# A slot-attention and feed-forward kernel: the first 520 pieces of its hand-written order, rearranged

## The chip, the cores and the metric

The kernel runs on one core of a Trainium2 chip. The metric is the device time of one execution in microseconds (us). TensorE (PE) multiplies matrices, VectorE (DVE), ScalarE (ACT) and GpSimd (POOL) do the element-wise work, and SyncE (SP) issues all the transfers (DMA). PEld is TensorE's loading of weights, which runs beside its products.

## What is computed

For each of 8 batches, 8 heads and 576 positions, phi (32 numbers) is turned into weights by a softmax. These weights pool k and v into 32 slots for each head; q attends to the slots, and the result, 4608 rows of 512, goes through a feed-forward layer.

```python
a = np.exp(phi - np.max(phi, axis=2, keepdims=True))
a = a / (np.sum(a, axis=2, keepdims=True) + 1e-09)
k_m = np.einsum('bhsm,bhsd->bhmd', a, k)
v_m = np.einsum('bhsm,bhsd->bhmd', a, v)
scores = scale * np.matmul(q, k_m.transpose(0, 1, 3, 2))
attn = softmax(scores)                      # over the 32 slots
x = rows of np.matmul(attn, v_m)            # 4608 x 512
h = x @ w_in                                # 4608 x 2048
out = (0.5 * h * (1.0 + erf(h / sqrt(2)))) @ w_out
```

## The kernel before

The whole program is a list of pieces, the string ORDER. Each word is a call, such as `h.0.3.1` or `dA.4.1:p`; a suffix after the colon picks the engine (d VectorE, a ScalarE, p GpSimd) or a PSUM pool (x, y). The pieces are traced in that order, and then every instruction is chained behind the one before it on its engine, so each engine works strictly in the order of the list. Engines wait for each other only where data or buffers ask for it.

Batch b's work is this. `Lphi`, `Lkv`, `Lkv0`, `Lq` load; `amax` and `aexp` (VectorE, ScalarE) do phi's softmax; `at` transposes it on TensorE and `atc` copies it out of PSUM; `slots.b.g.w` pools k (w 0) or v (w 1) for head group g; `km` scales the slots, `slotsT` transposes them and `kT` copies them. For batch 0 the scores are made in three parts: `n_score` (TensorE), `n_max`, `n_sub`, `n_exp`, `n_sum`, `n_inv`, `n_mul`, then `n_T` turns them and `n_hi` and `n_lo` split them into two parts, p_hi and p_lo. Later batches use `score`, `sT`, `max`, `sub`, `exp`, `sum`, `inv`, `mul`, `pT`, `ph`, `pl`. `Up.b.f.n` (line 695) multiplies v's slots by n blocks of 128 columns of w_in; `Uh` and `Ul` split the product into U. `h.b.f.half` (line 957, six products of 288 columns) gives 128 of the 2048 hidden units for half a batch; `gelu.b.f.half` (lines 965 to 968), `gh` and `gl` (line 974) follow, and `p.b.f` (line 988, twelve products of 512 columns) adds this block's share of the output into four PSUM banks, which `o.b.j.f` empties. `W.n` is n products of a block of ones (line 1058) whose result nobody reads.

The weights arrive as pairs of words and are decoded in the kernel. For block f, `.0` is w_in and `.1` is w_out: `Lwi.f` and `Lwo.f` load both into one tile raw_f; `dX` (lines 396 and 398) and `dY` (line 401) make two summands, `dA` adds them, and for w_out `dE` and `dF` split the sum into wo_hi and wo_lo.

```python
def dec_a(f, k):
    w, x = word_of(k, f), top_of(f, k).rearrange("p (c n) -> p c n", c=ND)
    e = eng("p")
    if e is nc.vector:
        w, x = upper(w), upper(x)
    e.tensor_tensor(w, w, x, op=ALU.add)
```

On VectorE an addition touches only the upper 16 bits; those of w_in lie 4 bytes apart, those of w_out 8, since `word_of` leaves w_out in raw_f.

Five buffers (the tag "U") serve the raw tiles and the U tiles, so that a load of block f waits until `dF` of an earlier block, or the last `h` of an earlier U, has let a buffer go. `h` has two PSUM buffers: an `h` waits for the gelu of the last but one. `score`, `Up`, `slots` and `at` of batch 1 share one pair of PSUM banks. phi has one buffer, so that batch 1's `Lphi` waits for the last `at` of batch 0.

Of the kernel before, what the change touches and what calls it, by code (L numbers as in the profile page):

```python
# [39 lines left out]
gelu.0.0.1 gh.0.0:a dY.3.1 Ul.0.2 gelu.0.1.1 dF.1 h.0.2.0 dY.2.1 Up.0.3.1 km.1.0:a gl.0.0  # L40
gh.0.1:a dA.3.1:p dX.2.1:d dY.4.1 gl.0.1 dX.4.0:a p.0.0 dX.4.1:d slots.1.1 dA.4.1:p
dE.3:a Lwi.5 h.0.2.1 dA.2.1:d Uh.0.3:a dY.4.0 Ul.0.3 Lq.1.0 dF.3 dE.2:a km.1.1:d slotsT.1
gelu.0.2.0 dE.4:a dY.5.0 kT.1:a Lwo.5 h.0.3.0 dA.4.0:d dX.5.0:d score.1.0 Lwi.7 dA.5.0:d
gelu.0.2.1 dF.4 gh.0.2:a sT.1.0.0 Lwi.6 gelu.0.3.0 Lq.1.1 h.0.3.1 sT.1.0.1 Lwo.6 Lphi.2.1
Up.0.4.2 max.1.0 p.0.1 dX.5.1:d Uh.0.4:a dY.5.1 gelu.0.3.1 dA.5.1:p sub.1.0 Ul.0.4
exp.1.0 h.0.4.0 dY.7.0 h.0.5.1 dE.5:a dF.2 gh.0.3:d gl.0.2 gelu.0.4.0 gelu.0.5.1
score.1.1 dX.6.1:a dY.6.0 dX.6.0:d p.0.2 dY.6.1 sum.1.0 dX.7.0:a gl.0.3 Lwo.8 h.0.5.0
Lwi.8 h.0.4.1 inv.1.0 dF.5 Up.1.0.4 gelu.0.5.0 gelu.0.4.1 mul.1.0 dA.6.0:p pT.1.0 dY.8.1
sT.1.1.1 Uh.1.0:a ph.1.0:a gh.0.4:a dA.6.1:p p.0.3 sT.1.1.0 dX.8.1:a dE.6:a dA.7.0:d
Lwo.7 max.1.1 Ul.1.0 gl.0.4 Up.0.6.2 Uh.0.6:a gh.0.5:d dY.7.1 sub.1.1 Ul.0.6 dX.7.1:a  # L50
dA.7.1:p gl.0.5 dF.6 p.0.4 exp.1.1 Lwo.9 h.0.6.1 Lwi.9 h.0.6.0 gelu.0.6.1 p.0.5 sum.1.1
pl.1.0 Lwi.11 h.0.7.1 dE.7:d dA.8.1:p gelu.0.6.0 inv.1.1 gelu.0.7.1 dY.9.0 h.1.0.0
dX.8.0:a Lwo.10 mul.1.1 h.0.7.0 gelu.1.0.0 gh.0.6:d gelu.0.7.0 pT.1.1 gl.0.6 ph.1.1:a
dY.8.0 Lwo.11 p.0.6 dF.7 Lwi.13 dX.9.1:d pl.1.1 gh.0.7:a dY.9.1 dX.9.0:a dA.9.1:p Lwi.10
gl.0.7 dE.8:d h.1.1.1 h.1.1.0 h.1.0.1 p.0.7 gelu.1.1.1 gelu.1.1.0 h.1.3.1 dY.11.0 dF.8
gh.1.1:d h.1.3.0 dA.8.0:d gl.1.1 dE.9:a h.1.2.1 gelu.1.0.1 o.0.2.7:a dX.11.0:d h.1.2.0
Up.1.4.4 gh.1.0:a dY.10.1 gelu.1.3.1 Lwo.14 dF.9 gl.1.0 dA.9.0:d gelu.1.3.0 o.0.0.7:a
dX.10.1:d o.0.3.7:d dY.10.0 o.0.1.7:a p.1.0 Lwo.13 dX.10.0:a dA.10.1:p gelu.1.2.1
gelu.1.2.0 dA.11.0:d Uh.1.4:a dE.10:a dA.10.0:d Ul.1.4 dY.14.1 dY.13.1 dY.11.1 h.1.7.1
h.1.4.1 Lwi.15 Up.0.8.4 Lwi.14 Lwi.12 p.1.1 dX.11.1:d dX.13.1:d dF.10 gh.1.2:a gl.1.2  # L60
Lwo.12 dY.15.0 dA.11.1:p p.1.2 Lphi.2.0 dX.13.0:d gelu.1.4.1 h.1.4.0 dX.14.0:d gh.1.3:a
h.1.5.1 dE.11:d h.1.5.0 gl.1.3 gelu.1.7.1 gelu.1.4.0 dY.14.0 gh.1.4:d p.1.3 gelu.1.5.0
gelu.1.5.1 h.1.7.0 gelu.1.7.0 Lwo.15 dF.11 h.1.6.1 dY.13.0 dY.12.0 gl.1.4 gh.1.5:d
Uh.0.8:a gl.1.5 gh.1.7:a h.1.6.0 Ul.0.8 dX.14.1:d dA.14.0:p p.1.4 gelu.1.6.0 dA.13.1:d
gelu.1.6.1 gl.1.7 p.1.5 h.0.8.1 gh.1.6:a gl.1.6 gelu.0.8.1 dX.12.0:d h.0.8.0 gelu.0.8.0
dY.12.1 h.0.10.0 p.1.6 dA.12.0:p h.0.9.0 dA.14.1:p dE.14:a p.1.7 h.0.10.1 h.0.9.1
dA.13.0:d dX.12.1:d Lkvu.2.0 gh.0.8:d h.0.11.0 dE.13:a dF.14 dA.12.1:p gelu.0.9.0 gl.0.8
o.1.1.7:a gelu.0.10.0 dE.12:a Lq.2.0 o.1.0.7:a gelu.0.10.1 dX.15.0:d o.1.2.7:d gelu.0.9.1
Up.0.12.2:x dA.15.0:d gh.0.9:a o.1.3.7:a gelu.0.11.0 amax.2.1 h.0.11.1 Uh.0.12:a gl.0.9
amax.2.0 dF.13 gelu.0.11.1 dX.15.1:a dF.12 dY.15.1 p.0.8 p.0.9 Ul.0.12 gh.0.10:d  # L70
h.0.12.1:y gh.0.11:a h.0.12.0:y h.0.13.0:x gelu.0.12.0 gl.0.10 gelu.0.12.1 h.0.13.1:x
dg.2 dA.15.1:d Up.0.14.2:y gl.0.11 gelu.0.13.0 gh.0.12:d Up.1.8.4:x p.0.10 gelu.0.13.1
Uh.1.8:a Uh.0.14:d gl.0.12 Ul.0.14 Ul.1.8 Lphin.2 gh.0.13:d p.0.11 h.0.14.0:y aexp.2.1
dE.15:a h.0.15.0:x h.0.14.1:y dF.15 aexp.2.0 h.1.8.0:y Lphi.3.0 Lphi.3.1 pn.2 gelu.0.14.0
gelu.0.14.1 gl.0.13 h.0.15.1:x gelu.0.15.0 h.1.8.1:y gelu.0.15.1 p.0.12 h.1.9.0:x
gh.0.14:d gh.0.15:d gl.0.14 gelu.1.8.0 gelu.1.8.1 aadd.2 anorm.2 Lkvu.2.1 gl.0.15 p.0.13
h.1.9.1:x gelu.1.9.0 p.0.14 gelu.1.9.1 gh.1.8:d gl.1.8 anexp.2 amax.3.0 amax.3.1 aexp.3.0
aexp.3.1 wg p.0.15 gh.1.9:d gl.1.9 dg.3 pn.3 h.1.10.0:y o.0.0.15 Lkv5.2 o.0.1.15
h.1.10.1:y gelu.1.10.0 o.0.2.15 h.1.11.0:x gelu.1.10.1 o.0.3.15 h.1.11.1:x gelu.1.11.0
# [1087 lines left out]
```

## Time and profile before

| | |
|---|---|
| median of 3 runs | 695.67 us (695.54 to 695.82) |
| profiled execution | 696.96 us, of which the span of its instructions is 695.2 us |
| TensorE busy in the span | 681.5 us (98%) |
| VectorE, ScalarE, GpSimd busy | 376.5, 298.8 and 40.0 us |
| TensorE's granted clock over the span | 0.996 of full speed |

Full speed is 2.4 GHz, and half of it, 1.2 GHz, is the other level. The busy time of TensorE is counted from modelled ends of its products, so a busy engine is not always at its peak. An engine's idle time costs something only if the work that sets the end waits for it.

### The profile page before, as it was taken

Reading aid. Unit: us, or ns where it says so; the run is one execution under the profiler, and the core shown is the slowest. Engines: PE = TensorE matmul, PEld = TensorE weight load, DVE = VectorE, ACT = ScalarE, POOL = GpSimd, SP = SyncE. Lnnn points to the kernel's source line nnn. Section 1 sums busy time; section 2 is a strip of 40 time slices with the busy share of each in tenths; the row PEclk is TensorE's granted clock in tenths of the full one; section 3 lists DMA queues with packets and bytes.
Section 4 is the critical chain, followed back from the end, with each engine's and each line's share of the span. In section 5 each row is a group of like instructions: output and inputs, shape, how many; then the busy total and the mean of one; then the engine's idle time right before and its main releaser. Section 6 shows DMA issues by size and latency. Waiting matters only on the chain.

```text
span 695.2 us, 12223 instructions
## 1 busy us (share of the span) xinstructions
PE 681.5 (98%) x4934; PEld 572.9 (82%) x4934; DVE 376.5 (54%) x708; ACT 298.8 (43%) x699; POOL 40.0 (6%) x31
## 2 busy tenths in 40 slices
...
GB/s 337 336 280 147 212 169 123 53 50 175 114 111 132 168 190 50 62 124 67 35 17 75 115 76 35 16 62 36 35 0 61 18 34 1 1 60 1 1 1 75
DMA packets 27865, 63.57 MB, mean 91 GB/s; under 512 B 2592, under 2 KB 6432, under 8 KB 27808
## 3 DMA queue, kind: packets, MB, share of 16 engines
...
q14 instruction: 18, 0.15, 0.1%
...
## 4 chain that ended last, share of the span: by engine, by line
PE 94%; DVE 2%; DMA 1%; ACT 1%; issue 0%; SPq 0%; DVEq 0%; ACTq 0%
PE acc L988 50%; PE h L957 29%; PE tacc L988 5%; PE pu L695 4%; PE psc L618 1%; PE psc L695 1%; DMA q<-qT 1%; PE pk L618 1%; PE psc L714 0%; PE pw L1058 0%; PE pk L603 0%; DVE U L316 0%; PE pt L524 0%; ACT L965 0%; DVE gl_t L983 0%
## 5 line engine op out<-in xcount | busy, mean ns | idle before, releaser
L957 PE MATMUL h<-p_hi,U 128*128 128x288 f32 x1024 | 217.2, 296 | 0.5 <-DVE U L316 0.3
L957 PEld LDWEIGHTS h<-p_hi,U 128*128 128x128 f32 x1024 | 168.7, 188 | 5.2 <-ACT gh L307 0.9
L988 PE MATMUL acc<-wo_hi,gh 128*128 128x512 f32 x512 | 161.2, 395 | 0.0
L307 DVE CAST gh<-gf 128x512 fp32r<-128x512 f32 x114 | 49.4, 433 | 204.5 <-PE acc L988 192.7
L988 PE MATMUL acc<-wo_lo,gh 128*128 128x512 f32 x512 | 158.6, 390 | 0.0
L988 PE MATMUL acc<-wo_hi,gl 128*128 128x512 f32 x512 | 158.6, 390 | 0.0
L957 PE MATMUL h<-p_lo,U 128*128 128x288 f32 x512 | 150.3, 295 | 0.0
L965 ACT ACTIVATE gf<-h 128x288 f32<-128x288 f32 x128 | 52.6, 412 | 174.2 <-PE h L957 149.7
L988 PEld LDWEIGHTS acc<-wo_hi,gh 128*128 128x128 f32 x512 | 92.9, 188 | 30.8 <-issue 14.7
L988 PEld LDWEIGHTS acc<-wo_hi,gl 128*128 128x128 f32 x512 | 96.1, 188 | 20.4
L988 PEld LDWEIGHTS acc<-wo_lo,gh 128*128 128x128 f32 x512 | 96.1, 188 | 19.2
L974 DVE TENSOR_TENSOR gl<-gf,gh 128x512 fp32r<-128x512 f32 x128 | 92.4, 722 | 32.9 <-PE acc L988 21.9
L957 PEld LDWEIGHTS h<-p_lo,U 128*128 128x128 f32 x512 | 96.1, 188 | 2.7
L967 ACT ACTIVATE gf<-h 128x224 f32<-128x224 f32 x128 | 45.8, 358 | 27.9 <-PE h L957 26.5
L316 DVE SCALAR_TENSOR_TENSOR U<-pu,U 128x512 fp32r<-128x512 f32 (+2 forms) x64 | 40.5, 682 | 5.6 <-ACT U L312 5.6
L312 ACT ACTIVATE U<-pu 128x512 fp32r<-128x512 f32 (+2 forms) x62 | 33.6, 610 | 11.6 <-PE pu L695 11.2
L695 PE MATMUL pu<-w_in_sb,kT 64*32 64x512 f32 (+2 forms) x592 | 33.8, 538 | 1.4 <-ACT kT L307 0.4
L968 ACT ACTIVATE tails<-h 128x64 f32<-128x64 f32 x128 | 28.8, 225 | 7.1 <-DVE gl_t L983 7.1
L307 ACT COPY raw_s<-psc 128x416 f32<-128x416 f32 (+1 forms) x12 | 5.6, 470 | 45.1 <-PE psc L695 45.1
L988 PE MATMUL tacc<-wo_hi,gh_t 128*128 128x512 f32 x64 | 24.9, 390 | 0.0
L988 PE MATMUL tacc<-wo_hi,gl_t 128*128 128x512 f32 x64 | 24.9, 389 | 0.0
L988 PE MATMUL tacc<-wo_lo,gh_t 128*128 128x512 f32 x64 | 24.9, 389 | 0.0
...
## 6 DMA issues: line engine op xcount, KB each, us to landing
...
```

What stands on the lines that cost most here:

```text
L307: return e.copy(dst, src) if e is nc.scalar else e.tensor_copy(dst, src)
L312: return e.activation(dst, src, AF.Copy, scale=W_SCALE)
L316: nc.vector.scalar_tensor_tensor(dst, src, W_SCALE, hi.bitcast(F32), op0=ALU.mult, op1=ALU.subtract)
L618: nc.tensor.matmul(pk[g][M * j : M * j + M], w[:, M * j : M * j + M], x[:, :, j, :], start=start, stop=stop,)
L695: nc.tensor.matmul(ps[g][M * j : M * j + M], st["kT", b][rows, t, M * j : M * j + M], moving[rows, j, :], start=True, stop=True,)
L957: nc.tensor.matmul(h[:, :HS], u[g][w], x[:, g, :], start=(n == 0), stop=(n == 3 * G - 1))
L965: nc.scalar.activation(gf[:, :HS], h[:, :HS], AF.Gelu)
L967: nc.scalar.activation(gf[:, HS:], h[:, : MAIN - HS], AF.Gelu)
L968: nc.scalar.activation(tails()[:, f, b % 2], h[:, MAIN - HS : HS], AF.Gelu)
L974: nc.vector.tensor_tensor(g_of("gl", b, f), g_of("gf", b, f), g_of("gh", b, f).bitcast(F32), op=ALU.subtract)
L988: nc.tensor.matmul(acc, x, w[:, f, :], start=(first and n == 0), stop=(last and n == 2))
```

## The change

Only ORDER changes, and in it only the first 514 pieces of 1716, which become 513; the other 1202 stay as they are. The same loads, products and element-wise steps are done. Four things differ:

- SyncE issues the first loads in another order: w_out's block 0 ahead of w_in's, one phi load of batch 1 ahead of both parts of q, w_in's block 1 and the values, and the other phi load behind them. Batch 1's q (`Lq.1.0`) moves ahead of `Lwi.4`.
- The products of ones were `W.4`, `W.3`, `W.1` and `W.8`, the last between `n_score.1` and `n_score.2`; now `W.8` stands ahead of `slotsT.0.0` and `n_score.0`, `W.4` behind `n_score.2` and `W.1` ahead of `slotsT.0.1`.
- Of the 32 additions `dA`, 18 were on GpSimd (5 of w_in, 13 of w_out) and 14 on VectorE (11 and 3); now 24 are on GpSimd (13 and 11) and 8 on VectorE (3 and 5).
- Some copies and roundings change between VectorE and ScalarE, and the order of pieces on every engine is another.

```diff
@@ -23,61 +23,61 @@
 ORDER = """
-Lphi.0.1 amax.0.1 Lphi.0.0 Lkv0.1.0 aexp.0.1 amax.0.0 aexp.0.0 Lkv0.0.0 at.0.1.0 Lwi.0
-at.0.1.4 Lq.0.0 at.0.0.0 at.0.0.4 Lwo.0 atc.0.1.4:d atc.0.0.0:a anorm.0 W.4 atc.0.1.0:d
-slots.0.1.0 Lphi.1.0 atc.0.0.4:a dX.0.0:a slots.0.0.0 Lphi.1.1 km.0.0.0:a dX.0.1:d
-km.0.1.0:a Lq.0.1 amax.1.1 Lwi.1 W.3 W.1 slotsT.0.0 kT.0.0:a Lkv0.0.1 dY.0.0 Lkv0.1.1
-dY.0.1 n_score.0 n_score.1 W.8 n_score.2 n_max.0 amax.1.0 aexp.1.1 n_sub.0 dX.1.0:d
-n_max.1 n_sub.1 dY.1.0 slots.0.0.1 aexp.1.0 n_exp.0 n_sum.0 n_exp.1 dA.0.1:p n_sum.1
-km.0.0.1:a n_inv.0 n_mul.0 dA.0.0:p Lwo.1 n_max.2 Lkv.1.0.4 n_inv.1 dE.0:d slots.0.1.1
-dA.1.0:p n_T.0 Lkv.1.0.1 km.0.1.1:a slotsT.0.1 kT.0.1:a n_sub.2 n_mul.1 Up.0.0.1 dX.1.1:d
-Lwi.3 dY.1.1 Uh.0.0:a n_exp.2 Lwi.2 Ul.0.0 n_T.1 n_hi.0:a Lkv.1.0.2 Lwo.3 n_sum.2
-Lkv.1.1.0 Lkv.1.1.2 Up.0.1.1 n_lo.0 Lwo.2 Uh.0.1:a Ul.0.1 dY.3.0 at.1.1.0 dY.2.0 n_inv.2
-at.1.0.0 Lkv.1.0.3 h.0.1.0 Lkv.1.0.0 n_mul.2 at.1.0.4 dX.2.0:d dF.0 at.1.1.4 n_T.2
-h.0.0.0 atc.1.1.0:a atc.1.0.0:a Lwo.4 dA.2.0:d dX.3.0:d gelu.0.1.0 atc.1.0.4:d dX.3.1:d
-dA.1.1:p atc.1.1.4:a n_hi.1:a Up.0.2.1 n_hi.2:d Lwi.4 Lkv.1.1.3 n_lo.2 n_lo.1 Lkv.1.1.1
-h.0.0.1 Lkv.1.1.4 h.0.1.1 slots.1.0 gelu.0.0.0 dE.1:a dA.3.0:d anorm.1 Uh.0.2:a
...
+Lphi.0.1 amax.0.1 Lphi.0.0 aexp.0.1 Lkv0.0.0 Lkv0.1.0 Lwo.0 amax.0.0 aexp.0.0 at.0.1.4
+Lwi.0 at.0.0.0 atc.0.0.0:a at.0.0.4 Lphi.1.0 atc.0.0.4:a anorm.0 Lq.0.0 at.0.1.0
+slots.0.0.0 atc.0.1.4:d dY.0.1 dX.0.0:a km.0.0.0:a Lq.0.1 atc.0.1.0:d Lwi.1 slots.0.1.0
+amax.1.0 km.0.1.0:d W.8 slotsT.0.0 dX.0.1:d kT.0.0:a dY.0.0 n_score.0 dA.0.1:p Lkv0.1.1
+n_max.0 n_sub.0 n_score.1 aexp.1.0 dY.1.0 Lkv0.0.1 n_score.2 dE.0:a W.4 n_exp.0 dX.1.0:d
+slots.0.1.1 n_max.1 n_sum.0 dA.0.0:p n_sub.1 slots.0.0.1 Lwo.1 dA.1.0:p n_inv.0 n_exp.1
+km.0.1.1:a n_max.2 n_mul.0 n_sum.1 W.1 Lphi.1.1 Lwi.2 Lwo.2 km.0.0.1:a slotsT.0.1 n_inv.1
+kT.0.1:a n_T.0 Lkv.1.1.2 Lkv.1.0.2 n_mul.1 n_sub.2 Lkv.1.0.1 dX.1.1:a Up.0.0.1 n_T.1
+Uh.0.0:a Up.0.1.1 Ul.0.0 n_hi.0:a n_exp.2 amax.1.1 Uh.0.1:d at.1.0.0 Ul.0.1 n_sum.2
+Lkv.1.1.1 n_lo.0 Lwi.3 dY.1.1 Lkv.1.0.3 aexp.1.1 dY.2.0 dX.2.0:a n_inv.2 Lkv.1.0.0
+n_mul.2 atc.1.0.0:a at.1.1.0 atc.1.1.0:d h.0.1.0 n_T.2 gelu.0.1.0 n_hi.1:d dF.0 at.1.0.4
+dA.1.1:p at.1.1.4 h.0.0.0 dA.2.0:p atc.1.0.4:a atc.1.1.4:a n_lo.1 n_hi.2:a dY.2.1
+Up.0.2.1 gelu.0.0.0 Uh.0.2:a n_lo.2 h.0.0.1 Lwo.3 anorm.1 dE.1:d h.0.1.1 dX.3.0:d Ul.0.2
+gelu.0.0.1 Lkv.1.0.4 dY.3.0 gh.0.0:a dX.2.1:d dX.3.1:d slots.1.0 gelu.0.1.1 Lwo.4
+km.1.0:d h.0.2.1 Lkv.1.1.0 Lkv.1.1.3 Lkv.1.1.4 gl.0.0 dA.3.0:p Up.0.3.1 Uh.0.3:d dY.3.1
+dA.2.1:p Ul.0.3 dE.2:a dY.4.1 p.0.0 dF.1 dX.4.1:a gh.0.1:a slots.1.1 Lq.1.0 dA.3.1:p dF.2
+km.1.1:d Lwi.4 dE.3:a h.0.2.0 gl.0.1 slotsT.1 h.0.3.1 gelu.0.2.1 Lwi.5 kT.1:d score.1.0
+dA.4.1:p gelu.0.2.0 dF.3 p.0.1 Lphi.2.1 dY.4.0 gh.0.2:d dX.4.0:d sT.1.0.0 Lwo.5 Lq.1.1
+h.0.3.0 sT.1.0.1 max.1.0 dE.4:a dX.5.0:d dY.5.0 dA.5.0:d sub.1.0 Lwo.7 dA.4.0:p gl.0.2
+Up.0.4.2 Lwi.6 dX.5.1:d p.0.2 exp.1.0 sum.1.0 dY.5.1 Uh.0.4:a gelu.0.3.0 Ul.0.4 score.1.1
+h.0.5.1 gelu.0.3.1 inv.1.0 dY.6.0 mul.1.0 h.0.4.1 h.0.4.0 dA.5.1:p pT.1.0 sT.1.1.1
+gelu.0.5.1 Lwi.7 dE.5:a sT.1.1.0 dF.4 Up.1.0.4 dX.6.0:a gh.0.3:d gl.0.3 Lwo.6 ph.1.0:a
+p.0.3 dY.7.0 dF.5 gelu.0.4.0 Uh.1.0:a gelu.0.4.1 h.0.5.0 dY.7.1 dX.7.0:d Ul.1.0 dA.6.0:d
+dY.6.1 dX.7.1:d gh.0.4:a gl.0.4 pl.1.0 dA.7.0:p Up.0.6.2 gelu.0.5.0 Uh.0.6:a p.0.4
+max.1.1 sub.1.1 Ul.0.6 Lwo.9 Lwi.9 dX.6.1:a exp.1.1 Lwi.8 gh.0.5:a dX.9.1:a sum.1.1
+dA.6.1:p h.0.6.0 Lwo.13 gl.0.5 Lwo.8 h.0.6.1 dE.6:d Lwi.13 gelu.0.6.0 inv.1.1 gelu.0.6.1
+mul.1.1 Lwi.11 dY.9.1 dF.6 dA.7.1:p Lwo.11 Up.1.4.4 pT.1.1 Lwo.10 gh.0.6:d ph.1.1:a p.0.5
+h.0.7.0 h.0.7.1 gelu.0.7.0 gelu.0.7.1 gh.0.7:a h.1.0.0 gl.0.6 dY.9.0 gl.0.7 h.1.1.0
+dA.9.1:p dX.8.0:a gelu.1.0.0 dE.7:a dE.9:a pl.1.1 dF.7 dX.8.1:a dF.9 p.0.6 dY.8.1
+dX.9.0:d h.1.1.1 gelu.1.1.1 p.0.7 dA.8.1:d dE.8:d dY.13.1 h.1.0.1 h.1.3.1 o.0.1.7:a
+gelu.1.1.0 Lwi.10 gh.1.1:d gl.1.1 h.1.3.0 h.1.2.1 dX.11.0:a gelu.1.0.1 gh.1.0:d gl.1.0
+Lq.2.0 gelu.1.3.1 o.0.3.7:d o.0.0.7:a gelu.1.3.0 Uh.1.4:d Lwo.12 Ul.1.4 h.1.2.0 dA.9.0:p
+p.1.0 p.1.1 o.0.2.7:a Lwi.12 dY.11.0 dY.10.0 dX.10.0:a dA.11.0:d gelu.1.2.0 dY.8.0 dF.8
+h.1.4.0 gelu.1.2.1 h.1.4.1 h.1.5.1 dY.13.0 dA.10.0:p dY.10.1 gh.1.2:a dX.13.1:d h.1.5.0
+gh.1.3:a gl.1.2 Lwi.15 Lwo.14 gl.1.3 gelu.1.4.0 dA.8.0:p Up.0.8.4 p.1.2 dX.10.1:d
+gelu.1.4.1 dY.11.1 gelu.1.5.1 dA.10.1:d dY.12.1 dX.11.1:a dE.10:d p.1.3 gelu.1.5.0
+dA.11.1:d dA.13.1:p dF.10 h.1.7.1 h.1.7.0 gh.1.4:d h.1.6.0 gelu.1.7.1 gelu.1.6.0 gl.1.4
+dE.11:d dX.12.0:a p.1.4 gh.1.5:d dF.11 h.1.6.1 gelu.1.7.0 Lphi.2.0 gl.1.5 dY.12.0 dY.15.0
+Lwi.14 p.1.5 dX.13.0:d gelu.1.6.1 dA.12.0:p Uh.0.8:a dX.14.0:a Lwo.15 dA.13.0:p gh.1.6:a
+Ul.0.8 dY.14.0 Lkvu.2.0 dX.14.1:d dX.15.0:a gh.1.7:a gl.1.6 gl.1.7 dY.14.1 dA.14.1:d
+dX.12.1:d h.0.8.0 h.0.10.0 p.1.6 h.0.8.1 gelu.0.8.0 Up.0.12.2:x h.0.9.0 gelu.0.8.1
+dA.14.0:p gh.0.8:d dE.14:a gelu.0.10.0 dA.12.1:d gl.0.8 h.0.10.1 p.1.7 h.0.9.1 amax.2.1
+gelu.0.9.0 amax.2.0 dE.12:a o.1.1.7:a o.1.0.7:a o.1.3.7:a gelu.0.10.1 dX.15.1:d h.0.11.0
+gelu.0.9.1 h.0.11.1 gh.0.9:a Uh.0.12:a dY.15.1 gl.0.9 dE.13:a p.0.8 gelu.0.11.0 dF.12
+o.1.2.7:d Ul.0.12 dA.15.0:p gh.0.10:d gelu.0.11.1 h.0.12.0:y dF.14 h.0.12.1:y gh.0.11:a
+gl.0.10 dF.13 p.0.9 h.0.13.0:x h.0.13.1:x gelu.0.12.1 gelu.0.12.0 gelu.0.13.0 Up.0.14.2:y
+Up.1.8.4:x gelu.0.13.1 gl.0.11 gh.0.12:d Uh.0.14:d Uh.1.8:a dg.2 Ul.0.14 Ul.1.8 Lphin.2
+gh.0.13:d dA.15.1:p p.0.10 dE.15:a p.0.11 gl.0.12 h.0.15.1:x h.0.14.1:y dF.15 h.0.14.0:y
...
```

## Rows read from the trace of the kernel before

**Rows 1.** Busy time by stretch; stretch, length, each engine's busy us, clock, DMA.

```profile
10.00:20.00 10.00, 6.53 (x46) 6.21 (x47) 4.37 (x8) 5.25 (x13) 3.78 (x3) 0.89 1.02 398
20.00:30.00 10.00, 8.14 (x153) 6.71 (x152) 8.37 (x23) 4.97 (x13) 1.29 (x1) 0.94 1.01 367
30.00:40.00 10.00, 9.14 (x114) 7.11 (x113) 8.13 (x22) 9.90 (x24) 2.36 (x2) 1.00 0.68 228
60.00:140.00 80.00, 79.75 (x512) 67.01 (x511) 52.36 (x83) 50.23 (x111) 15.66 (x10) 1.00 0.41 138
```

**Rows 2.** The chain that ended last, 5 to 24 us: start, length, what.

```profile
8.35 8.11 DMA q<-qT
...
16.59 2.51 PE psc L714 x16
19.10 2.93 PE pw L1058 x16
22.03 0.84 PE psc L714 x8
```

**Rows 3.** Timeline of TensorE, first 36 us: start, length, line, output, operands.

```profile
7.24 1.06 PE L1058 MATMUL pw<-one 128*128 128x128 f32 x8
8.23 1.73 PE L591 MATMUL pk<-w_in_sb,aT 128*32 128x64 f32 x80
11.88 1.97 PE L714 MATMUL psc<-k_blocks,q 128*128 128x128 f32 x16 [0.72 <-ACT k_blocks L307]
22.80 1.73 PE L591 MATMUL pk<-w_in_sb,aT 128*32 128x64 f32 x80
29.57 0.38 PE L957 MATMUL h<-p_hi,U 128*128 128x288 f32 x1
```

**Rows 4.** Timeline of the transfers' issues, first 24 us.

```profile
7.50 0.80 SPq L432 DMA_DIRECT2D phi<-phiT  x2
21.33 1.80 SPq L443 DMA_DIRECT2D kv<-kv  x2
```

**Rows 5.** SyncE's own waits: total us, times, longest.

```profile
SPq L443 <- DMA w_in_sb<-kv: 1.8, 1, 1.8
```

**Rows 6.** Timelines of VectorE and ScalarE in the start.

```profile
15.05 0.75 DVE L492 TENSOR_REDUCE nm<-phi 128x1 f32<-128x576 f32 x1 [1.72 <-DMA phi<-phiT]
...
9.40 0.78 ACT L396 ACTIVATE top<-raw 128x512 f16<-128x512 bf16 x1 [1.32 <-DMA raw<-w_in]
11.25 0.53 ACT L307 COPY k_blocks<-tn 64x128 f32<-64x128 f32 x2 [0.70 <-PE tn L658]
```

**Rows 7.** Steps of the decoding: ns min/median/max, first and last start us.

```profile
L316 DVE SCALAR_TENSOR_TENSOR wo_lo<-raw,wo_hi x16: 628/682/1736, 29.7 to 136.8; 128x512 fp32r<-128x512 f32 x16
...
L416 POOL TENSOR_TENSOR raw<-raw,top x13: 1275/1337/1957, 14.6 to 111.9; 128x512 int32<-128x512 int32 x13
L416 DVE TENSOR_TENSOR w_in_sb<-w_in_sb,top x11: 729/754/1701, 30.3 to 115.9; 128x512 int16<-128x512 int16 x11
...
L416 DVE TENSOR_TENSOR raw<-raw,top x3: 1312/1324/1330, 38.8 to 124.0; 128x512 int16<-128x512 int16 x3
```

**Rows 8.** Timeline of all engines around 48 us.

```profile
48.16 1.30 POOL L416 TENSOR_TENSOR raw<-raw,top 128x512 int32<-128x512 int32 x1 [7.02 <-ACT raw L401]
...
48.27 1.74 DVE L316 SCALAR_TENSOR_TENSOR wo_lo<-raw,wo_hi 128x512 fp32r<-128x512 f32 x1
```

**Rows 9.** Groups by form, 33 to 141 us: busy us, mean ns, idle before.

```profile
L965 ACT ACTIVATE gf<-h 128x288 f32<-128x288 f32 x23 | 9.4, 415 | 6.8 <-PE h L957 4.1 <-DVE gl L974 2.6
...
L316 DVE SCALAR_TENSOR_TENSOR U<-pu,U 128x1024 fp32r<-128x1024 f32 x3 | 3.7, 1225 | 4.3 <-ACT U L312 4.3
L307 ACT COPY part<-acc 128x512 f32<-128x512 f32 x6 | 3.5, 587 | 2.0 <-PE acc L988 2.0
```

**Rows 10.** Timeline of TensorE around 45 us.

```profile
44.92 0.40 PE L957 MATMUL h<-p_hi,U 128*128 128x288 f32 x1
...
46.11 0.67 PE L695 MATMUL pu<-w_in_sb,kT 64*32 64x256 f32 x16
```

48 lines of the change are left out of this document (7 added, 41 removed).

## The prediction

> **What bounds the kernel now.** I read the busy times by stretch first [rows 1]. From 60 to 140 us TensorE is busy for 79.75 of 80 us, and its own work does not change, so from there on the kernel can win nothing and can only lose by new pauses. TensorE's slack lies ahead of 40 us: it is busy for 6.53, 8.14 and 9.14 of 10 us in the three stretches from 10 to 40 us, 6.2 us idle in all, and its granted clock averages 0.89 and 0.94 in the first two, so some of the work there ran at 1.2 GHz. The chain says what sets the order of that start [rows 2]: the second part of batch 0's q (`Lq.0.1`), issued at 8.35 us, lands at 16.46; then come `n_score.1` (2.51 us), the block of ones `W.8` (2.93) and `n_score.2` (0.84), and only then the products that pool v, at 22.80 [rows 3]. From there the first `h` is 6.8 us away, at 29.57 [rows 3]. The ones, whose result nobody reads, thus stand in the middle of the chain.
>
> **The start, step by step.** Transfers land in the order of issue. I add their sizes from the shapes (phi 288 KB, first k or v 576, a weight block 512, q 512 and 640) and take the landing times that the trace shows: w_in's block 0, 2240 KB into the list, at 9.40 [rows 6]; the second phi load, 3840 KB, at 15.05 [rows 6]; q's second part, 4480 KB, at 16.46 [rows 2]; the last values, 6144 KB, at 21.33, where the transfer eight places behind them is let go (a wait of 1.8 us) [rows 4, 5]. In the new list batch 1's first phi load ends at 3040 KB, q's second part at 4192, the values at 5280 and 5856. Between the points above that is 12.2, 15.8, 18.8 and 20.5 us. One caution: batch 1's phi still waits for the last `at`, as it did at 7.50 us [rows 4], and now q, w_in's block 1 and the values queue behind it on SyncE; 2752 KB are ahead of it, so I expect no dry spell.
>
> `amax.1.0` now stands ahead of `km.0.1.0` on VectorE. It waits for that phi (12.2) and takes 0.75 us [rows 6]; with an allowance of 0.3 us each for `km` and `slotsT`, smaller than the 0.53 of the copy to k_blocks that follows [rows 6], `n_score.0` starts at about 14.3 us instead of 11.88 [rows 3]. That is a loss of 2.4 us, but a covered one: `n_score.1` could not start before q's second part anyway. At full clock a score block of 16 products takes 1.97 us [rows 3], so `n_score.0` ends at 16.3, `n_score.1` at 18.2, `n_score.2`, half as long, at 19.2. `W.4`, 1.06 us for its 8 products [rows 3], ends at 20.3. The values' products follow at 20.3 instead of 22.80: **2.5 us sooner**. The first group's values have landed by then (18.8), the second's land at 20.5, while the first group's products run (1.73 us for both [rows 3]). Behind them come the same steps as before, so `h.0.1.0` starts at about 27.1 and the steady part 2.5 us sooner. Bounds: 0.8 us if the clock falls in the new pauses (below); 3.5 us if phi lands a microsecond sooner than I interpolate. I take 2.5, since each term is a row's.
>
> Batch 1's q, ahead of `Lwi.4` now, is hidden on both sides: in the part before it TensorE has no wait for q beyond the one of the chain, so I cost it at nothing; if it were late, `score.1.0` would be.
>
> **The additions.** VectorE had 11 of w_in at 0.754 us and 3 of w_out at 1.324 [rows 7], 12.3 us; it keeps 3 and 5, 8.9 us. It is relieved of 3.4 us although five dear ones come to it. GpSimd gets six more, at 1.34 us each [rows 7], 8 us on an engine that is busy for 15.66 of 80 [rows 1]. So the additions as such cost nothing on the path, where VectorE is busy for 52.36 of 80 us [rows 1]. What they do to each other is the second rival.
>
> **Pauses that go.** Between `h.0.3.1` and `Up.0.4.2` lie 1.19 us [rows 10], where the six products of an `h` take 0.8 by the gaps between neighbouring ones. In the new order `p.0.1` stands between, and `Up.0.4.2` has more time for its operands. I credit 0.4 us.
>
> **Pauses that come.** I followed each `h` to the gelu that frees its buffer, and each `p` to its `gl` and to the evictions of its banks. Four places look too tight:
>
> 1. `Up.0.6.2` needs `dA.6.0`, now behind `Ul.1.0` on VectorE. Those two take 1.23 and 0.75 us [rows 7, 9], and `Uh.1.0` ahead of them stands behind four decoding steps on ScalarE; only `p.0.3` and `h.0.5.0` cover that. I put 0.5 us (0 to 2.0, the two steps whole), and 0.2 for `h.0.6.0`, whose `Ul.0.6` stands behind `pl`, `max` and `sub`.
> 2. `h.1.3.1` and `h.1.3.0` need the buffers of `h.1.1.0` and `h.1.0.1`. Their gelus stand on ScalarE behind `dX.8.1`, `dY.8.1`, an eviction and `dX.11.0`, and block 11 can't be loaded before `dF.7` frees a raw buffer. One `dX` is 0.78 us [rows 6]; I put 0.6 (0 to 2).
> 3. `h.0.11.0` needs `gelu.0.10.1`, which now stands behind three evictions of batch 1's first half on ScalarE. The last of them must wait for the end of `p.1.7`; it takes 0.59 us and the gelu 0.42 [rows 9] and its tail, against 0.8 of `h.0.9.1` as cover. I put 0.7 with the like wait of `h.0.10.1` (0.2 to 1.5).
> 4. `o.1.2.7` is on VectorE behind `gl.0.9` and `dF.12`, whereas `p.0.8` wants that bank at once; and `h.0.12.0` needs `gelu.0.11.0` behind two decoding steps. 0.5 us (0 to 1.5).
>
> Sum: 2.5 us. These are the places where I chose; the bounds are 0.2 and 7.
>
> **The sum.** 2.5 + 0.4 - 2.5 leaves 0.4 us won. As the middle of the pauses' bounds is the less certain part and several of them may partly fall into one another (a pause in one place gives the late engine time at the next), I take 0.8 us. The profiled execution took 696.96 us for a span of 695.2, 1.3 us above the median of the runs; counted from the median of 695.67 the forecast is 694.9 us. What a measurement of this kernel can tell from no change is 0.2%, 1.4 us, so the forecast is that no difference shows.
>
> **The rivals.**
>
> *The start's gain stays whole.* The four pauses shrink because the buffers come free as early as the start does. For it: ScalarE and VectorE are busy for 50.23 and 52.36 of 80 us [rows 1], so there is room to catch up. Against it: each pause is a matter of order, not of load. Then 2.5 + 0.4 less 0.5 of pauses: 693.3 us. It decides from pauses under 1.5 us.
>
> *GpSimd's additions hold VectorE up; slower.* A `dF` that started 0.1 us into an addition on GpSimd took 1.74 us instead of the median of 0.68 [rows 7, 8]: 1.06 us more. Six more additions on GpSimd give up to six more such blocks, 6.4 us of VectorE time against the 3.4 spared. Between 20 and 40 us VectorE is busy for 8.37 and 8.13 of 10 us [rows 1], and a block of `dF.1` there also delays the next raw buffer. If three of six reach TensorE on top of the pauses above, the time is 694.9 + 3.2 = 698.1. It decides from two blocks on the path. By the Trainium skill ("SBUF — State Buffer", Who interferes with whom) the two engines share a pair of ports under an exclusive lock, and an operation with both inputs in SBUF waits for the whole instruction of the other; the trace agrees in that row.
>
> *The clock falls again in the start.* In the kernel before, TensorE waited until 16.59 us for q [rows 2], and its clock then fell: `n_score.1` took 2.51 us where `n_score.0` took 1.97 [rows 2, 3], and the 16 instructions of `W.8` 2.93, where 8 of `W.4` took 1.06 [rows 2, 3]. The new order has pauses of about 1.4 and 0.7 us ahead of `n_score.0`, with one transposition between; before, the pause was longer and in one piece. If it falls there, three score blocks and `W.4` lose some 1.7 us: 696.6 us.
>
> *The reordered loads change nothing*, because data ends all of it and lands as before: start gain 1, pauses 2.5, 696.8. The chain speaks against it: 2.93 us of ones leave it.
>
> **How the numbers follow.** Chances: the forecast 0.42, the whole gain 0.24, GpSimd's blocks 0.14, the clock 0.14, nothing 0.06. Of the forecast's own range, 693.6 to 696.3, a quarter lies below 694.28, the bound of faster. Faster: 0.10 + 0.24, and 0.02 from the rest: 0.36. Slower (above 697.06): 0.11 of GpSimd's blocks, 0.05 of the clock, 0.02 of the last, 0.02 of the forecast: 0.20. Same: 0.44. The range reaches from the whole gain with its start at the upper bound, 692.8, to 697.6, between the clock's case and the blocks'; a tenth is left out on each side.
>
> **What would show it.** Right: q's second part lands near 15.8 us, v's products start near 20.3 and the first `h` near 27; no ones between the score blocks. The four pauses would stand as idle time or as long gaps ahead of `Up.0.6.2`, `h.1.3.0`, `h.0.11.0` and `h.0.12.0`. Wrong: the first `h` later than 28.5 us; a granted clock of 0.5 after 14 us; many `dF` or `gl` far above 0.7 us; waits of `h` or `p` in places that I did not name.

## The result, and the profile after

The changed kernel takes 700.52 us (median of 5 runs, 699.68 to 701.36), beside 695.82 us for the kernel before on the same chip (5 runs, 695.54 to 696.74). The ratio is 1.0066, with a 95% interval of 1.0047 to 1.0085: slower by 4.7 us. The prediction, 694.9 with a range of 692.8 to 697.6, was wrong, and the sign of its forecast too.

The profiled execution is the fastest of the five: 699.68 us, a span of 697.9, which is 2.7 us more than the 695.2 of the execution profiled before. Its windows, with the columns of [rows 1]:

```profile
10.00:20.00 10.00, 8.65 (x102) 7.93 (x99) 3.88 (x8) 5.42 (x11) 3.24 (x3) 0.90 0.98 378
20.00:30.00 10.00, 7.11 (x142) 5.34 (x142) 8.07 (x22) 7.76 (x16) 3.22 (x3) 0.95 1.01 389
30.00:40.00 10.00, 9.89 (x113) 7.90 (x112) 8.02 (x20) 6.58 (x20) 4.26 (x3) 0.88 0.60 179
60.00:140.00 80.00, 79.19 (x504) 65.97 (x503) 53.47 (x82) 49.51 (x110) 19.09 (x13) 1.00 0.41 139
24.00:29.00 5.00, 2.13 (x41) 1.25 (x32) 4.14 (x12) 4.94 (x12) 1.87 (x2) 1.00 1.05 410
29.00:32.40 3.40, 3.40 (x16) 3.31 (x16) 2.46 (x6) 1.73 (x4) 0.77 (x1) 0.50 0.34 110
```

Between 10 and 20 us TensorE is busier than before (8.65 against 6.53 us), as was meant. But between 20 and 30 us it is less busy (7.11 against 8.14), and the stage from 30 to 40, all at full clock before, has a mean clock of 0.88: after five microseconds with only 2.13 of work, the clock stands at one half for 3.4 us, just where the first `h` run. From 60 to 140 us TensorE has lost another 0.56 us. The chain that ended last, from 7 to 32 us (start, length, what):

```profile
7.93 5.32 DMA phi<-phiT
...
15.39 4.65 PE psc L714 x40
20.04 0.95 PE pw L1058 x8
...
28.22 0.57 ACT aT L307
...
28.84 0.99 PE pt L524 x4
29.83 1.44 PE h L957 x6
```

The beginning goes nearly as forecast: batch 1's phi lands at 13.25 us, the three score blocks run from 15.39 without a break, and the products that pool v start at 20.91 instead of 22.80 [rows 3], 1.9 us sooner. Yet `h.0.1.0` starts at 29.48, where it started at 29.57 before [rows 3], and takes 1.59 us to the next piece instead of 1.46. At `slots.1.0` nothing of the gain is left. Its first products, and those that pool v, in the trace of after:

```profile
20.91 1.73 PE L591 MATMUL pk<-w_in_sb,aT 128*32 128x64 f32 x80
...
35.20 1.07 PE L603 MATMUL pk<-kv,aT 128*32 128x128 f32 x30
```

and those of `slots.1.0` in the trace of before:

```profile
35.23 0.97 PE L603 MATMUL pk<-kv,aT 128*32 128x128 f32 x28
```

To find the rest, I took for each piece on TensorE the time from its first product to the next piece's first, less the shortest such time of its kind. What is left over is a pause (or half clock); below 0.18 us it counts as none. A change from one kind of product to another can also show in it: the 0.23 us of `p.0.0` and ahead of `Up.0.6.2` before are a `p` with another kind behind it, and no wait.

| place | forecast, us | before | after |
|---|---|---|---|
| `h.0.3.1` to `Up.0.4.2` | goes, 0.4 | 0.39 | none |
| ahead of `Up.0.6.2`, `h.0.6.0` | 0.7 | 0.23 | none |
| ahead of `h.1.3.0` | 0.6 | none | 0.68 |
| ahead of `h.0.11.0`, `h.0.10.1` | 0.7 | none | 0.42 |
| `p.0.8`, `h.0.12.0` | 0.5 | none | none |
| in `p.0.0` | not named | 0.23 | 0.59 |
| ahead of `h.1.8.0` | not named | 0.42 | 1.20 |

From `slots.1.0` to `p.1.9`, where the two orders have become one, TensorE needs 130.24 us instead of 127.50: 2.7 us, the whole difference of the two spans. The rows of the table that differ make 1.6 of it; the rest lies in many gaps of 0.25 us or less, which I did not follow one by one. The median has lost 2 us more than the profiled pair shows; the runs below tell where.

### The profile page after: what moved, and what is told of

The parts are those of the page before. It is cut to its first block, busy times and chain, and to the rows that moved or that the text cites. A ratio compares the mean times of both kernels' runs of the same rounds, so it can differ in the third digit from the quotient of the medians.

```text
span 697.9 us, 12213 instructions
## 1 busy us (share of the span) xinstructions
PE 683.5 (98%) x4928; PEld 573.2 (82%) x4928; DVE 377.1 (54%) x705; ACT 297.4 (43%) x696; POOL 46.9 (7%) x37
## 4 chain that ended last, share of the span: by engine, by line
PE 92%; DVE 3%; ACT 2%; DMA 1%; issue 1%; DVEq 0%; ACTq 0%
PE acc L988 49%; PE h L957 28%; PE tacc L988 5%; PE pu L695 4%; PE psc L618 1%; PE psc L695 1%; DMA phi<-phiT 1%; DMA raw<-w_in 1%; PE psc L714 1%; PE pk L618 1%; DVE U L316 1%; PE pk L603 0%; DVE gl L974 0%; DVE gl_t L983 0%; DVE nm L492 0%
## 5 line engine op out<-in xcount | busy, mean ns | idle before, releaser
L307 DVE CAST gh<-gf 128x512 fp32r<-128x512 f32 x115 | 50.8, 442 | 202.1 <-PE acc L988 192.4
L312 ACT ACTIVATE U<-pu 128x512 fp32r<-128x512 f32 (+2 forms) x59 | 31.7, 610 | 12.0 <-PE pu L695 10.6
L551 POOL PARTITION_ALL_REDUCE pn<-dg x6 | 11.3, 1884 | 214.3 <-DVE dg L546 103.1
```

The costliest lines, as they stand in the source:

```text
L307: return e.copy(dst, src) if e is nc.scalar else e.tensor_copy(dst, src)
L312: return e.activation(dst, src, AF.Copy, scale=W_SCALE)
L551: nc.gpsimd.partition_all_reduce(pn.rearrange("p g n -> p (g n)"), st["dg", b].rearrange("p g n -> p (g n)"), P, bass_isa.ReduceOp.add,)
```

## The experiments

"Theory A" is that waits made by the order are the whole loss; "theory C" that the granted clock in the start is a large part. Each kernel was timed beside the kernel before, whose median in the five groups lay between 695.62 and 696.64 us. The clock is TensorE's mean granted clock, averaged over the runs.

| run | median, us | ratio to before | clock |
|---|---|---|---|
| changed kernel | 700.52 | 1.0047 to 1.0085 | 0.994 |
| e1_at_swap | 699.24 | 1.0027 to 1.0060 | 0.996 |
| e2_h14_first | 699.35 | 1.0030 to 1.0063 | 0.995 |
| e4_old_start | 698.87 | 1.0025 to 1.0052 | 0.998 |
| e5_new_start | 698.90 | 1.0026 to 1.0052 | 0.993 |
| e6_more_ones | 699.25 | 1.0032 to 1.0060 | 0.999 |
| e7_middle | 699.56 | 1.0037 to 1.0078 | 0.994 |
| e8_all | 696.45 | 0.9996 to 1.0022 | 0.998 |
| e9_before_ones | 696.29 | 0.9993 to 1.0021 | 0.997 |
| e10_before_more_ones | 697.79 | 1.0009 to 1.0037 | 1.000 |
| e11_additions | 697.28 | 1.0018 to 1.0039 | 0.999 |
| e12_km_first | 696.80 | 0.9995 to 1.0019 | 0.998 |
| e13_old_engines | 712.84 | 1.0192 to 1.0245 | 0.986 |
| e14_before_few_ones | 696.35 | 0.9988 to 1.0018 | 0.998 |

### Start and middle apart

`e4_old_start` takes the pieces up to `slots.1.0` in the order of before and all others in the new one; `e5_new_start` is the counterpart.

> The pieces up to slots.1.0 in the order of the kernel before, all other pieces in the order of the changed kernel. Theory A (the start is worth nothing, the pauses of the middle are worth 2.7 us of the profiled span): slots.1.0 at about 35.2 us, p.1.9 at about 178.6 as in the changed kernel, median 698.4 to 699.5. Theory C (the start of the changed kernel also makes the runs differ among themselves, by another fall of the clock, and that is the rest of the 4.7 us between the medians): the runs lie within 1 us of each other and the median is about 698.5. If the middle alone makes the whole difference: 700.5.

> The counterpart: the pieces up to slots.1.0 in the order of the changed kernel, all other pieces in the order of the kernel before (without the products W.3). Theory A (the start is worth nothing): slots.1.0 at about 35.2 us, p.1.9 at about 176, median 695.5 to 696.3. Theory C (the start costs some runs another fall of the clock): the profile is as in theory A, but the runs differ by over 1 us and the median is 697 to 698. My prediction's own step (the start is worth 2.5 us): 693.3.

Each half alone costs about as much: 2.8 us for the new middle and 2.8 for the new start, 1.7 to 3.6 by either interval. (The sum is more than 4.7, which these intervals allow; ahead of `h.1.3.0`, where block 11 is late, the sooner start of `e4_old_start` lost 1.16 us instead of 0.68.) So the start is not worth nothing, as the pair of traces had suggested, but dear. That is theory C, although not in its figures: the runs of `e4_old_start` differ by 2.2 us and not by 1, and the median of `e5_new_start` is 0.9 us above the 697 to 698. With the new start `slots.1.0` came at 35.20, 37.30, 38.17 and 36.22 us in four executions (after, e2, e5, e7); with the old one at 35.23, 33.92 and 33.97 (before, e4, e11).

The trace of before had caught an execution with a fall of the clock, that of after the fastest of its five. In `e4_old_start` the same first pieces, `n_score.1`, `W.8`, `n_score.2` and the products that pool v, ran at full clock:

```profile
16.18 1.97 PE L715 MATMUL psc<-k_blocks,q 128*128 128x128 f32 x16 [1.54 <-DMA q<-qT]
17.98 2.00 PE L1059 MATMUL pw<-one 128*128 128x128 f32 x16
19.82 1.00 PE L715 MATMUL psc<-k_blocks,q 128*128 128x128 f32 x8
20.76 1.73 PE L592 MATMUL pk<-w_in_sb,aT 128*32 128x64 f32 x80
```

So the products that pool v start at 20.76 us here, and at 21.00 in `e11_additions`, in the old order and with the ones in their old place. The 22.80 of the trace of before were those of a fall at 17.85 us, and against the old start at full clock the new one, at 20.91, had won nothing even there.

In `e5_new_start` (windows as above):

```profile
24.00:29.90 5.90, 3.77 (x72) 2.31 (x60) 5.33 (x15) 4.93 (x13) 1.30 (x1) 1.00 1.05 406
30.00:36.80 6.80, 6.12 (x39) 5.38 (x40) 4.37 (x15) 4.32 (x11) 1.32 (x1) 0.50 0.47 140
```

Here the half clock lasts 6.8 us, through nearly all the first `h` (31.45 to 38.17 us).

### The wait of the transpositions

Here and below, the diffs show only the words that change and their neighbours.

```diff
-n_mul.2 atc.1.0.0:a at.1.1.0 atc.1.1.0:d h.0.1.0
+n_mul.2 at.1.1.0 atc.1.0.0:a atc.1.1.0:d h.0.1.0
```

The changed kernel's timeline at the place (start, length, engine, line; what ended the idle time in brackets):

```profile
26.96 0.63 PE L524 MATMUL pt<-ident,phi 128*128 128x128 f32 x4 [1.12 <-DVE U L316]
...
27.03 0.67 ACT L401 ACTIVATE w_in_sb<-raw 128x512 int32<-128x512 uint32 x1
...
27.59 0.77 ACT L396 ACTIVATE top<-raw 128x512 f16<-128x512 bf16 x1
...
28.22 0.56 ACT L307 COPY aT<-pt 128x512 f32<-128x512 f32 x1
...
28.84 0.99 PE L524 MATMUL pt<-ident,phi 128*128 128x128 f32 x4 [1.25 <-ACT aT L307]
...
29.48 0.59 PE L957 MATMUL h<-p_hi,U 128*128 128x288 f32 x1
```

`at.1.1.0` waits for the copy of `at.1.0.0`, whose pair of banks it shares, and the copy stands on ScalarE behind two decoding steps of block 2. Before, both transpositions stood ahead of both copies.

> Changed kernel with two neighbours of the list exchanged: at.1.1.0 now stands ahead of atc.1.0.0, so the second group of transpositions need not wait for the copy that empties the first (both lie in one pair of PSUM banks). No engine's own order changes. Theory A (the start's gain was lost in that wait): at.1.1.0 starts at about 27.4 us instead of 28.84, the first h at about 28.0 instead of 29.48, slots.1.0 at 33.5 to 34 instead of 35.20; the median goes from 700.5 to about 699.0, and to 697.3 if the clock then does not fall at 29 us. Theory B (the fall of the clock at 29.02 us ate the gain): the first h comes sooner, but TensorE still falls to half clock between 26 and 31 us and slots.1.0 stays within 0.5 us of 35.2; the median stays within 0.7 us of 700.5.

The eight transpositions now run as one group:

```profile
27.86 1.59 PE L524 MATMUL pt<-ident,phi 128*128 128x128 f32 x8 [1.12 <-DVE U L316]
29.11 0.59 PE L957 MATMUL h<-p_hi,U 128*128 128x288 f32 x1
```

From `Up.0.0.1` to `h.0.1.0` it takes 4.36 us instead of 5.63. (The first `h`, at 29.11 us, is later than theory A's 28.0, but the values' products had begun 0.9 us later in this execution than in that of after.) The clock fell nevertheless (at 28.24 us), and `slots.1.0` came at 34.65. The median is 1.3 us lower, but the intervals overlap; by the trace the wait is shown, by the clock both theories have a share.

### Ones in the waits

```diff
-W.8 slotsT.0.0
+W.8 slotsT.0.0 W.3
-Up.0.0.1 n_T.1
+Up.0.0.1 n_T.1 W.2
-Uh.0.1:d at.1.0.0
+Uh.0.1:d W.4 at.1.0.0
-at.1.1.0 atc.1.1.0:d
+W.4 at.1.1.0 atc.1.1.0:d
```

> Changed kernel with 13 more products of ones in four places where TensorE waits: W.3 behind slotsT.0.0, W.2 behind n_T.1, W.4 ahead of at.1.0.0 and W.4 ahead of at.1.1.0. Nothing else changes. Theory C (the start is lost to the granted clock, which falls at 28 to 30 us behind a stretch in which TensorE mostly waits): no half clock between 24 and 36 us, the first h takes 0.8 to 1.0 us of its own instead of 1.4, slots.1.0 starts at 33.3 to 34 us instead of 35.2 to 37.3, and the median falls by 1.5 to 2.5 us from 700.5, to 698 to 699. Theory A (the waits themselves are the loss): the waits stand in the same places with or without the ones, slots.1.0 at 35 us or later, median within 0.7 us of 700.5.

```profile
24.00:29.00 5.00, 4.90 (x64) 3.78 (x61) 4.50 (x12) 4.96 (x12) 1.36 (x2) 1.00 1.05 410
29.00:32.40 3.40, 3.04 (x37) 2.62 (x37) 2.43 (x7) 3.08 (x8) 1.28 (x1) 1.00 0.30 112
```

The same stretches as in the trace of after, TensorE busy for 4.90 us instead of 2.13, and no half clock; all five runs have a mean clock of 0.999 or 1. But `slots.1.0` came at 34.45 us, not at 33.3 to 34, and the median fell by 1.3 us only, within overlapping intervals. So the ones hold the clock, and even so the new start is later than the old one at full clock (33.92). The wait of the transpositions is still in it: from the values' products to `h.0.1.0` it takes 8.35 us, as against 8.57 in the trace of after and 7.12 in that of `e4_old_start`. Theory C explains a part.

### The pauses of the middle

```diff
-p.0.11 gl.0.12 h.0.15.1:x h.0.14.1:y dF.15 h.0.14.0:y
+p.0.11 gl.0.12 h.0.14.0:y h.0.15.1:x h.0.14.1:y dF.15
```

In the changed kernel, ahead of `h.1.8.0`:

```profile
139.53 0.68 DVE L974 TENSOR_TENSOR gl<-gf,gh 128x512 fp32r<-128x512 f32 x1
...
140.28 1.28 ACT L965 ACT_TABLE_LOAD   x1 [3.73 <-DVE gl L974]
...
141.57 0.41 ACT L965 ACTIVATE gf<-h 128x288 f32<-128x288 f32 x1
...
142.03 0.40 PE L957 MATMUL h<-p_hi,U 128*128 128x288 f32 x1 [1.04 <-ACT gf L965]
```

ScalarE's first gelu there is `gelu.0.14.0`, but `h.0.14.0` had become the third `h`. When its products are through, at about 140.2 us, the table load (1.28 us) and the gelu follow, and only one `h` of 0.8 us is left as cover. The row names a `gl` on VectorE that ended at the same time; that is `gl.0.13`, which this gelu does not need (`gl.0.12` was through at 139.0 us), so the order of the `h` has to be changed to tell the two apart.

> Changed kernel with h.0.14.0 as the first of the four h behind p.0.11 instead of the third, since gelu.0.14.0 is the first gelu behind them on ScalarE. Theory A (the order of the h makes the pause of 1.2 us ahead of h.1.8.0): the table load and gelu.0.14.0 start 1 to 1.5 us sooner, the pause falls to 0.2 us or less, and the profiled span from p.0.11 on is 1.0 us shorter (of 700.5, about 699.5). Theory B (VectorE is late with gl.0.12, whose buffer gelu.0.14.0 overwrites): the table load starts at about 139.1 us instead of 140.28 and a pause of 0.5 us or more stays, or moves to the next h.

The pause falls from 1.20 to 0.29 us, near what theory A says; the load now waits for VectorE (141.11 us, `gl.0.12`), which accounts for what is left. This execution's start was 2.1 us later than that of after; the median is 1.2 us lower, within overlapping intervals.

```diff
-dX.11.0:a gelu.1.0.1 gh.1.0:d gl.1.0 Lq.2.0 gelu.1.3.1 o.0.3.7:d o.0.0.7:a gelu.1.3.0
+gelu.1.0.1 gh.1.0:d gl.1.0 Lq.2.0 gelu.1.3.1 o.0.3.7:d o.0.0.7:a gelu.1.3.0 dX.11.0:a
-o.1.0.7:a o.1.3.7:a gelu.0.10.1
+o.1.0.7:a gelu.0.10.1 o.1.3.7:a
-dA.2.1:p
+dA.2.1:d
```

The first edit's place in the changed kernel; block 11 is requested at 75.26 us, when `dF.7` is done, and ScalarE waits for it with two gelus queued behind:

```profile
80.28 0.79 ACT L396 ACTIVATE top<-raw 128x512 f16<-128x512 bf16 x1 [0.89 <-DMA raw<-w_in]
...
81.16 0.21 ACT L968 ACTIVATE tails<-h 128x64 f32<-128x64 f32 x1
...
81.43 0.41 PE L957 MATMUL h<-p_hi,U 128*128 128x288 f32 x1 [0.52 <-ACT tails L968]
```

The third edit's place; `gl.0.0` overlaps `dA.2.1`, and `p.0.0` waits for it:

```profile
36.87 3.02 POOL L416 TENSOR_TENSOR raw<-raw,top 128x512 int32<-128x512 int32 x2
36.97 1.75 DVE L974 TENSOR_TENSOR gl<-gf,gh 128x512 fp32r<-128x512 f32 x1
```

> Changed kernel with three edits of the part behind the start: dX.11.0 behind gelu.1.3.0 instead of ahead of gelu.1.0.1 (ScalarE waits in it for block 11's transfer), gelu.0.10.1 ahead of the last of three evictions, and dA.2.1 on VectorE as before (on GpSimd it overlapped gl.0.0, which took 1.75 us instead of 0.69). Theory A (each pause is one of order): the pause ahead of h.1.3.0 (0.7 to 1.2 us in the runs so far) and that ahead of h.0.11.0 (0.42) go, and p.0.0 takes 2.9 to 3.0 us instead of 3.3; together 1.4 to 1.9 us from slots.1.0 to p.0.8, median about 699.0. Theory B (the engines or the transfers are late as such): at least two of the three come back within the next ten products (as a wait of p.0.0 for gl.0.0 behind VectorE's addition, of h.1.2.1 or h.1.5.1, of p.0.8 for the eviction), and the gain stays below 0.6 us.

`p.0.0` takes 2.95 us, so that edit holds. The pauses ahead of `h.1.3.0` and `h.0.11.0` are gone too, but the gain was given back. `p.0.8` took 3.07 us, 0.35 more than the shortest: it waits for `o.1.2.7` on VectorE, the prediction's fourth place, which the pause ahead of `h.0.11.0` had covered. And block 10 came late in this execution:

```profile
87.92 0.67 ACT L401 ACTIVATE w_in_sb<-raw 128x512 int32<-128x512 uint32 x1 [2.87 <-DMA raw<-w_in]
...
94.22 0.40 PE L957 MATMUL h<-p_hi,U 128*128 128x288 f32 x1 [2.66 <-ACT gf L965]
```

So in this execution the transfers of that stretch are late as such, and the order only decides which `h` waits: theory B there. It is not the usual one: the profiled run took 702.75 us and another 702.87, the other four 698.52 to 699.69, and no other profile has a pause above 1.2 us in that stretch.

### All repairs together

`e8_all` has the edits of e1, e2 and e7 and the ones of e6 without those ahead of `at.1.1.0`; `e12_km_first` adds one exchange.

```diff
-amax.1.0 km.0.1.0:d
+km.0.1.0:d amax.1.0
```

> All repairs of the changed kernel in one: the exchange of at.1.1.0 and atc.1.0.0, h.0.14.0 first, dX.11.0 later, gelu.0.10.1 sooner, dA.2.1 on VectorE, and 9 more products of ones (behind slotsT.0.0, behind n_T.1 and ahead of at.1.0.0). If the clock (theory C) and the pauses (theory A) are the whole cause: slots.1.0 at 32.5 to 33.5, p.1.9 at about 174.5, median 694.5 to 696, below or level with the kernel before. If something else costs (the loads of the new order, say): 697 or more.

> The changed kernel with all repairs (the exchange at at.1.1.0, h.0.14.0 first, the three edits of the middle, nine more products of ones) and now also km.0.1.0 ahead of amax.1.0 on VectorE, so that the first scores do not wait for batch 1's phi. My prediction holds that wait to be covered by the wait for q: then n_score.1 starts at 17.0 us or later as without the edit and nothing changes, median 696.4. Rival (q has long landed; the wait for phi is on the path): n_score.0 at about 13 us instead of 15.1, n_score.1 at 15.0 to 15.8, v's products at 19.0 to 19.8 instead of 20.65, unless the values end it, and the median is about 695.4.

`e8_all` is level with the kernel before and 4 us below the changed kernel; here the intervals do not overlap. But the two halves are not repaired alike. In the start, at full clock from 12 us on, it takes 6.88 us from the values' products to `h.0.1.0`, and `slots.1.0` comes at 33.04 us: 2.2 us sooner than in the trace of before, and 0.9 sooner than the old start at full clock. There the wait and the clock are the whole loss, and in this execution a small gain lies under them. From `slots.1.0` to `p.1.9` it takes 129.41 us, and before 127.50: of the 2.7 us lost there only 0.8 came back. The pauses have moved rather than gone: 0.57 and 0.55 us ahead of `h.1.0.1` and `h.1.3.1`, where ScalarE waits 2.93 us for block 8's words with their gelus behind, and 0.35 us in `p.0.8`.

```profile
75.58 0.79 ACT L396 ACTIVATE top<-raw 128x512 f16<-128x512 bf16 x1 [2.93 <-DMA raw<-w_out]
```

The median of `e12_km_first`, 696.80 us, is no different. In it, TensorE in the start:

```profile
15.16 1.97 PE L714 MATMUL psc<-k_blocks,q 128*128 128x128 f32 x16 [0.54 <-DMA q<-qT]
17.80 2.36 PE L714 MATMUL psc<-k_blocks,q 128*128 128x128 f32 x19 [0.68 <-DMA q<-qT]
```

Without the wait for phi ahead of them both score blocks wait for q. My prediction's "covered loss" holds here, but for a reason that it did not see. The loads of q in the kernel before (their number, first and last issue, then the time to landing), and in the changed one:

```profile
L476 SPq DMA_DIRECT2D q<-qT x2: 432/474/516, 3.1 to 8.3; - x2
...
DMA to landing us min/median/max: 8.1/8.3/8.4
```

```profile
L476 SPq DMA_DIRECT2D q<-qT x2: 431/432/433, 8.3 to 8.8; - x2
...
DMA to landing us min/median/max: 6.3/6.9/7.5
```

q's first part, issued at 3.1 us before, now stands behind the phi load that waits for the last `at`, and leaves at 8.3. The second lands at 8.8 + 7.5 = 16.3 us, where it landed at 16.46 before [rows 2]. The new order of loads brought q no sooner.

### The ones in the kernel before

```diff
-n_score.0 n_score.1 W.8 n_score.2
+n_score.0 W.8 n_score.1 n_score.2
```

> The kernel before with one word moved: W.8 stands ahead of n_score.1 instead of behind it, in the 2.7 us in which TensorE waits for the second part of q. This does only what my prediction took for the source of the start's gain: the ones leave the chain from q to the first h. By the prediction's step: n_score.1 starts at 16.6 as before, the products that pool v at 20.3 instead of 22.8 unless the values come later, the first h about 2 us sooner, median 693.5 to 694.5. Theory C (ones matter where they stand for the clock): no fall at 17.85, which gives 1 us more in some runs, but a fall may come at 24 to 30 instead. Rival: what follows is bound by the transfers (block 1 of w_in, batch 1's phi and values), and the first h stays at 29 us or later: median 695.5 to 696.5.

> The kernel before with W.8 ahead of n_score.1 (as in the run before) and 16 more products of ones where TensorE waits: W.3 behind slotsT.0.0, W.2 behind slots.0.0.1 and slotsT.0.1, W.1 behind n_T.1, W.4 behind Up.0.1.1, W.2 behind h.0.1.0 and h.0.0.0. Theory C (with W.8 moved alone, runs with a mean clock of 0.998 or more took 694.7 to 695.8 us and those below 696.8 to 698.8; the clock decides): the mean clock is 0.998 or more in nearly all runs and the median 694.5 to 695.2, 1 us or so below the kernel before. Theory A (only waits count): no change against W.8 moved alone, 696.3, and the same scatter of 4 us.

> The kernel before with W.8 ahead of n_score.1 and only two more groups of ones, W.2 behind slotsT.0.1 and W.4 behind Up.0.1.1, in waits of 0.57 and 1.06 us that are longer than the products (0.5 and 1.0 us). Theory C (with W.8 moved alone, half of the runs lose 2 us to the clock, which falls in the stretch of short waits behind the values' products; the 16 products of the larger set cost time themselves): the mean clock is 0.997 or more in nearly all runs, the median 694.7 to 695.3, below the kernel before. Rival (the clock falls elsewhere, or the ones there cost what they save): scatter as before with W.8 moved, median 696 or more.

In the profiled execution of `e9_before_ones`, which has no fall of the clock in the start, the step that the prediction counted on is there, from one moved word:

```profile
14.22 2.00 PE L1058 MATMUL pw<-one 128*128 128x128 f32 x16
16.26 2.86 PE L714 MATMUL psc<-k_blocks,q 128*128 128x128 f32 x24
19.05 0.90 PE L591 MATMUL pk<-w_in_sb,aT 128*32 128x64 f32 x40
20.58 0.90 PE L591 MATMUL pk<-w_in_sb,aT 128*32 128x64 f32 x40 [0.63 <-DMA w_in_sb<-kv]
```

The values' products start at 19.05 us, the first `h` at 27.31, and the run took 694.69 us. Against the old start at full clock that is 1.7 us at the values' products and only 0.5 at the first `h` (27.88 and 27.76 us in e4 and e11). And of twelve runs the six with a mean clock of 0.998 or more took 694.67 to 695.75 us, and the six below it 696.82 to 698.77; the median is that of before. With more ones (`e10_before_more_ones`) the clock holds (0.9995), but the median is higher by 2.2 us; whether the ones' own time costs that is not shown, since q also landed 1.8 us later in its profiled execution. With only six more (`e14_before_few_ones`) the median is 696.35 us beside 696.64, no difference. No version here beats the kernel before.

### The additions

`e11_additions` is the kernel before with the new engines of the additions, `e13_old_engines` the changed kernel with the old ones. In each, 18 words change, in the first as these do and in the second the other way round:

```diff
-dA.2.0:d
+dA.2.0:p
-dA.6.0:p
+dA.6.0:d
```

> The kernel before, its own order, with only the engines of the additions as in the changed kernel: 18 of 32 change places between GpSimd and VectorE. My prediction costs this at nothing. If GpSimd's additions hold VectorE up on the path (the rival): 2 to 3 us more than the kernel before, 698 to 699, with VectorE steps of 1.2 us or more over their median beside GpSimd's additions and more of them than the ten in the trace of before (8.4 us in all). If a single block matters (gl.0.0, which took 1.75 us beside dA.2.1 in the changed kernel and made p.0.0 0.4 us longer): 0.3 to 0.8 us more, 696.3 to 696.8.

> The changed kernel, its own order, with only the engines of the additions as in the kernel before. In the order of before, the new engines cost 1.7 us, by the trace because dA.6.0 came to VectorE ahead of the transposition sT.1.1.0, which Up.1.0.4 waits for; that is a matter of that order. Theory A (the engines fit the order they were placed for): the changed kernel gets no faster, 700 to 701.5; p.0.0 is 0.3 us shorter, since gl.0.0 no longer runs beside dA.2.1, and a new pause of 0.5 us or more comes elsewhere. Rival (GpSimd's additions cost the changed kernel the 1.7 us too): 698.5 to 699.2.

The new engines cost the old order 1.3 to 2.7 us. In the trace of `e11_additions`:

```profile
53.94 0.79 DVE L416 TENSOR_TENSOR w_in_sb<-w_in_sb,top 128x512 int16<-128x512 int16 x1 [0.65 <-ACT w_in_sb L401]
54.61 0.77 DVE L863 STREAM_TRANSPOSE pT<-sT 128x576 f32<-128x576 f32 x1
...
55.48 0.85 DVE L807 STREAM_TRANSPOSE sT<-psc 128x288 f32<-128x288 f32 x2
```

`dA.6.0`, now on VectorE, waits there for ScalarE, with the transposition behind it that empties the banks for `Up.1.0.4` (a wait of 0.81 us). VectorE instructions that take over 0.5 us more than their kind's median beside an addition number 10 up to 145 us, against 8 before.

The old engines in the new order cost 12 us, far more than theory A's 700 to 701.5. One of the places:

```profile
38.51 1.75 POOL L416 TENSOR_TENSOR raw<-raw,top 128x512 int32<-128x512 int32 x1 [10.34 <-DVE km L644]
39.03 1.81 DVE L416 TENSOR_TENSOR w_in_sb<-w_in_sb,top 128x512 int16<-128x512 int16 x1
```

`dA.3.0` on VectorE takes 1.81 us instead of 0.75 beside an addition on GpSimd, and `Up.0.3.1` waits 1.90 us for it. The clock also fell three more times, at 42.0, 69.3 and 151.2 us; how much of the 12 us that makes is not shown. Each set of engines does better with its own order; the rival, that the new engines cost the changed kernel 1.7 us, has fallen.

## Why the prediction was wrong

**The start** is the step that failed: "Behind them come the same steps as before, so `h.0.1.0` starts at about 27.1 and the steady part 2.5 us sooner." Up to the values' products the terms held: 20.91 us against 20.3, and the 0.6 us are the later phi (13.25 against 12.2, behind which `n_score.0` came 2.1 us later, as reckoned) less the shorter score blocks. But the steps behind them were not the same. The order of transposition and copy had been exchanged at `at.1.1.0`, a wait of 1.25 us that I did not look for, and half clock followed TensorE's thin work in that stretch. From the values' products to `h.0.1.0` I had 6.8 us; in the six profiles with the exchanged pair and the new start (after, e2, e5, e6, e7, e13) it took 8.35 to 8.90, in the three that put the pair back (e1, e8, e12) 6.88 to 7.30. With the changed kernel's start and no more ones the clock fell between 27.9 and 30 us in all six profiles (after, e1, e2, e5, e7, e13); in the four of the old start (before, e4, e9 with `W.8` moved, e11) it never did there, and fell at all only in that of before, at 17.85 us. By the runs the start costs 2.8 us where 2.5 were forecast as a gain.

**The base** of that gain was wrong too. I saw in the rows that the clock had fallen in `n_score.1` and `W.8`, and still took the 22.80 us behind them as the kernel's own. At full clock the old start reaches that point at 20.76 and 21.00 us (e4, e11), so that even the forecast 20.3 was a gain of 0.5 to 0.7 us and not of 2.5. And I took the 2.5 from the median of 695.67 us, which lies 1.3 us below the traced execution, about what the fall cost it: `slots.1.0` at 35.23 us, and at 33.92 and 33.97 without a fall.

**The clock** was my third rival, at 14%. Its mechanism came true, its place only in part: I looked ahead of `n_score.0` (e2 and e5 had half clock around it, from 15 and 16 us), and not at the wait-ridden stretch from 24 to 29 us, which the trace of before also has.

**q.** Its second part was to land at 15.8 us; it landed at 16.3. I had noted that q would queue behind phi's wait and expected no harm; the first part left 5 us later for it.

**The pauses** were sized rightly as a sum and wrongly one by one, so that the sum is in part luck. Forecast: 2.5 less 0.4; in the trace 2.7, by `e4_old_start` 2.8. Two of the four named places came (0.68 for 0.6, 0.42 for 0.7) with the causes given; of the other two one did not, and one was covered by the pause ahead of it until `e7_middle` took that away (0.35); two that I had not named (0.78 and 0.36 us more than before) and many small ones made up for them. Where `e7_middle` and `e8_all` took pauses away, others came in their place. At `h.1.8.0` the method would have found it: I paired each `h` with its own gelu, and not with the first gelu on ScalarE.

**GpSimd's additions**, the second rival: the added blocks did not come. Of VectorE's instructions up to 145 us, 8 were over 0.5 us above their kind's median beside an addition before (7.6 us in all), 6 after (6.2 us). One of them reached TensorE, in `p.0.0`. "The additions as such cost nothing" is not a fact of the additions: in the old order the same engines cost 1.7 us, and in the new order the old ones 12.

**Left open:** what sets the place and length of the half clock from one execution to the next; the 1.1 us of small gaps in the middle; and why more ones made the kernel before slower.
